# One condition for the pairs and singles that rarely run, and two weight pieces behind the last tile's divisions

## The chip, the cores and the metric

The kernel runs on one core of one Trainium2 chip. The metric is the device time of one launch in microseconds (us), as the median of several runs. The core's engines are named as in the profile: PE is TensorE (matmuls; PEld its weight loads), DVE is VectorE, ACT is ScalarE, POOL is GpSimd and SP is SyncE, which issues most DMA transfers.

## The reference

One sequence of 2048 tokens with 512 features goes through two blocks, each behind a layer norm without weights, each added to its input. The first is linear attention with 32 heads of 16 features and a learned feature map (two softmaxes per head). The second is a mixture of 8 experts, of which each token takes one:

```python
h = x + _A_ref(_layernorm(x, axis=-1), A_wqkv, A_w_phi, A_wo)
h2 = h + _B_ref(_layernorm(h, axis=-1), B_w_gate, B_w1, B_w2)
```

```python
logits = xf @ w_gate
topk_idx = jnp.argsort(-logits, axis=-1)[:, :K]      # K = 1
gates = _softmax(topk_val, axis=-1)                  # of one value
...
h = _silu(xf @ w1[e]) @ w2[e]                        # 512 -> 1792 -> 512
out = out + w * h
```

All is float32. The kernel computes an expert for the tokens routed to it only. How many those are is known when the router has run: with these inputs 103, 594, 80, 127, 286, 222, 239 and 397.

## The kernel before

**Precision.** A float32 value is split into a high part (line 89, ScalarE copies it into a shorter format) and a low part (line 92, or 252 for weights: VectorE subtracts the high part from the value). A product is three matmuls: high by high (L95), high by low (L96), low by high (L97). So each weight chunk that arrives costs one pass of ScalarE and one of VectorE, and each group of matmuls reads both.

**Stages.** The profile's order of time is: attention's features up to about 177 us; the output stage up to about 265; and the experts. The output stage is a loop over 16 tiles of 128 tokens, with its steps staggered: `s_num` (attention's numerator and denominator, divided on VectorE at L573 and L574 into `o`), `s_ot` (transposes of `o` into the bank `pto`, split into `xh` and `xl`), `s_wo` (output projection, bank `po`; then `hb`, the sum with the input, and `lg`, the logits; its statistics at L1022 and L1025 on ScalarE with `hnm` on POOL between them), `s_rank` and `s_inv` (place of each token in its expert, `ivT`). The first expert's weights are already split in that loop, in quarter pieces (`hi_piece`, `lo_piece`); the table `LOS` says in which round of the loop the low pieces of a chunk come.

**Experts.** The largest expert's tokens go as one unit of 128 and one wide group of 468, a second and a third expert in wide groups of 400 and 288 (WN). What is left goes in pairs (up to 256 rows of one expert, two tiles of 128) and singles (128 rows). The program's order is: unit 0, wide group of 468, pair 1, pair 2, pairs 3 to 8 if there are so many, WN, single 0, wide group of 400, single 1, singles 2 to 7 if there are so many. With these inputs two pairs and three singles are live, so pairs 3 to 8 are jumped over and single 2 runs inside its condition. A conditional block is fallen into where it runs; where it doesn't, each engine compares and jumps behind it.

**Preparing the next unit.** A unit makes the next one ready while it runs: it gathers its rows from DRAM (`rows`, `gather`; POOL, L180), normalizes them (`ahead`, VectorE, L207), transposes them on TensorE (`turned`, L214, tile `mtr`) and splits the result (`xhi`, `xlo`); it also splits the next weight chunks (`step`, `split`) and asks for the ones behind (`fetch`, `load`, on SP). Where the next unit may not exist, `split` and `fetch` stand under small conditions on flags that each engine loads into a register (`load_fl`, `load_flags`). Since pair q may be followed by another pair, each pair does this for pair q + 1 with no condition on the transposes, and `keep(q)` stores what the result of pair q needs: the row numbers, and the rows themselves in a second pair of buffers. The result (`pair_result`, L1424) is written by the unit that comes next.

**What sets the order.** The program is written once; a scheduler orders each engine's instructions by the durations that it expects and by explicit ties (`after(x)`: issue not before x; `pin` holds the last instruction of a kind). So an instruction moved in the text can reorder its neighbours on other engines. A bank of PSUM is reused in turn: a matmul into a bank waits for the engine that reads the bank's earlier content.

## Time and profile before

| | us |
|---|---|
| median of 3 runs | 620.19 (619.78 to 621.09) |
| profiled execution | 619.78 |
| its span, first to last instruction | 618.0 |
| mean granted clock of TensorE | 0.998 |
| busy in the span: TensorE | 609.5 |
| VectorE | 441.6 |
| ScalarE | 354.5 |
| GpSimd | 240.5 |

A line of a timeline reads: start in us, duration in us, engine, line of the kernel, operation, tile written <- tiles read, shape, and in brackets the idle time of the engine ahead of it with what ended it. Matmuls overlap in the pipeline, so the cost of one is best read from one start to the next. A line of waits gives engine, operation and line, what it waited for, the total in us, how often, and the longest. In a table of windows each engine has its busy time in the window.

### The profile page before, as it was taken

Reading aid. Unit: us, or ns where it says so; the run is one execution under the profiler, and the core shown is the slowest. Engines: PE = TensorE matmul, PEld = TensorE weight load, DVE = VectorE, ACT = ScalarE, POOL = GpSimd, SP = SyncE. Lnnn points to the kernel's source line nnn. Section 1 sums busy time; section 2 is a strip of 40 time slices with the busy share of each in tenths; the row PEclk is TensorE's granted clock in tenths of the full one; section 3 lists DMA queues with packets and bytes.
Section 4 is the critical chain, followed back from the end, with each engine's and each line's share of the span. In section 5 each row is a group of like instructions: output and inputs, shape, how many; then the busy total and the mean of one; then the engine's idle time right before and its main releaser. Section 6 shows DMA issues by size and latency. Waiting matters only on the chain. (4 is left out here: it accounts for less than half of the span.)

```text
span 618.0 us, 13816 instructions
## 1 busy us (share of the span) xinstructions
PE 609.5 (99%) x5213; PEld 545.4 (88%) x5213; DVE 441.6 (71%) x938; ACT 354.5 (57%) x626; POOL 240.5 (39%) x333
## 2 busy tenths in 40 slices
PE   9999999999999999999999999999999999999996
PEld 8888888888889999888888898888899889999885
DVE  7988787878898878886534557776555784346893
ACT  6666676667535546873234546666456655645771
POOL 3577688868716645541110022240301430010440
PEclk9999999999999999999999999999999999999999
DMA  8711111110103249531078267574755594444931
GB/s 317 264 37 53 52 52 53 54 53 19 36 4 99 74 150 399 206 109 56 21 275 326 69 239 313 200 251 151 248 196 175 174 336 157 136 171 141 326 127 39
DMA packets 25121, 95.12 MB, mean 154 GB/s; under 512 B 3838, under 2 KB 3838, under 8 KB 17873
## 3 DMA queue, kind: packets, MB, share of 16 engines
q1 hardware_dynamic: 20624, 80.81, 37.0%
q0 software_dynamic: 4272, 13.28, 6.4%
q8 instruction: 44, 0.72, 0.5%
q14 instruction: 37, 0.29, 0.1%
q10 hardware_dynamic: 144, 0.02, 0.0%
HBM read 85.68 MB, written 8.65 MB: 153 GB/s over the span
## 5 line engine op out<-in xcount | busy, mean ns | idle before, releaser
L252 DVE TENSOR_TENSOR wlo<-raw,whi 128x1024 fp32r<-128x1024 f32 (+1 forms) x119 | 135.2, 1159 | 29.4 <-ACT whi L89 28.4
L89 ACT ACTIVATE whi<-raw 128x1024 fp32r<-128x1024 f32 (+1 forms) x120 | 115.2, 992 | 8.2 <-DMA raw<-in_w_dram 5.1
L180 POOL DMA_INDIRECT xg<-hbuf,gidx x26 | 34.1, 1312 | 126.4 <-DVE xn L207 48.6
L95 PE MATMUL gw<-zx,whi 128*128 128x240 f32 (+3 forms) x212 | 69.6, 328 | 0.9 <-issue 0.7
L97 PE MATMUL gw<-zx,wlo 128*128 128x240 f32 (+3 forms) x212 | 68.1, 321 | 0.0
L96 PE MATMUL gw<-zx,whi 128*128 128x240 f32 (+3 forms) x212 | 68.1, 321 | 0.0
L711 POOL TENSOR_TENSOR ph<-t,sm 128x1024 f32<-128x1024 f32 x32 | 62.1, 1942 | 12.6 <-DVE sm L709 12.3
L92 DVE TENSOR_TENSOR hA<-hs,hA 128x240 fp32r<-128x240 f32 (+3 forms) x57 | 26.7, 469 | 50.4 <-ACT hA L89 49.1
L1376 ACT ACTIVATE hs<-gw 128x468 f32<-128x468 f32 (+2 forms) x39 | 19.2, 491 | 72.4 <-PE gw L97 72.4
L95 PE MATMUL yt<-hA,whi 128*128 128x468 f32 (+2 forms) x168 | 56.7, 338 | 0.0
L97 PE MATMUL yt<-hA,wlo 128*128 128x468 f32 (+2 forms) x168 | 56.7, 338 | 0.0
L703 ACT ACTIVATE t<-t,rstd 128x1024 f32<-128x1024 f32 x32 | 36.9, 1152 | 34.0 <-DVE t L702 31.0
L708 DVE TENSOR_REDUCE sm<-t 128x64 f32<-128x1024 f32 x32 | 38.8, 1212 | 7.4 <-ACT t L703 5.3
L95 PEld LDWEIGHTS gw<-zx,whi 128*128 128x128 f32 x212 | 39.9, 188 | 3.6 <-ACT hs L1376 1.0
L96 PEld LDWEIGHTS gw<-zx,whi 128*128 128x128 f32 x212 | 40.0, 189 | 1.4
L97 PEld LDWEIGHTS gw<-zx,wlo 128*128 128x128 f32 x212 | 39.9, 188 | 1.3
L95 PE MATMUL po<-wohi,xh 128*128 128x260 f32 x128 | 37.5, 293 | 0.6 <-DVE cum L1045 0.6
L96 PE MATMUL yt<-hA,whi 128*128 128x288 f32 (+2 forms) x116 | 37.8, 325 | 0.0
L97 PE MATMUL po<-wohi,xl 128*128 128x260 f32 x128 | 36.5, 285 | 0.0
L96 PE MATMUL po<-wolo,xh 128*128 128x260 f32 x128 | 36.1, 282 | 0.0
L89 ACT ACTIVATE hA<-hs 128x240 fp32r<-128x240 f32 (+3 forms) x70 | 33.4, 478 | 2.2
L197 POOL DMA_INDIRECT out_dram<-xg,sidx x12 | 14.4, 1202 | 50.1 <-DVE xg L1401 28.2
(490 smaller groups left out, 1783.1 us busy)
## 6 DMA issues: line engine op xcount, KB each, us to landing
raw<-in_w_dram SPq DMA_DIRECT2D x56, 1024.0 KB
xt<-in_x_dram SPq DMA_DIRECT2D x32, 256.0 KB
xT<-in_xTs_dram SPq DMA_DIRECT2D x16, 256.0 KB
hbuf<-hb SPq DMA_DIRECT2D x6, 515.0 KB
hbuf<-hb SPq DMA_DIRECT2D x2, 514.0 KB
phT<-in_wv_dram SPq DMA_DIRECT2D x4, 256.0 KB
phT<-in_wqkT_dram SPq DMA_DIRECT2D x4, 256.0 KB
phT<-in_wqkT_dram SPq DMA_DIRECT2D x2, 512.0 KB
```

Of the source, the lines that this page charges most:

```text
L89: return A.activation(dst, src, AF.Copy)
L92: return V.tensor_tensor(dst, src, hi.bitcast(F32), op=OP.subtract)
L95: T.matmul(ps, ahi, bhi, start=first, stop=False)
L96: T.matmul(ps, ahi, blo, start=False, stop=False)
L97: return T.matmul(ps, alo, bhi, start=False, stop=last)
L180: G.indirect_dma_start(out=dst[0:n, :], out_offset=None, in_=hbuf if col or tab is gidS else hbuf[0:S // 2, :], in_offset=bass.IndirectOff ...
L197: m = G.indirect_dma_start(out=out, out_offset=bass.IndirectOffsetOnAxis(ap=tab[0:n, col:col + 1], axis=0), in_=src[0:n, 0:D], in_offset=N ...
L252: return eng.tensor_tensor(lo, r, h.bitcast(F32), op=OP.subtract)
L703: pin["ex"] = A.activation(t, t, AF.Exp, scale=st[c]["rstd"])
L708: V.tensor_reduce(sm, t, AX.X, OP.add)
L711: pin["f2"] = G.tensor_tensor(ph.rearrange("p (a f) -> p a f", f=DH), t, bc(sm, DH), op=OP.mult)
L1376: A.activation(h, p, AF.Silu)
```

## The change

Three things change. Pairs 3 to 8 and singles 3 to 7 go together into one outer condition at the program's end; single 2 loses its condition (it now always runs), and the late pairs become a plain function, `late_pair`, that prepares nothing ahead. Since no pair follows pair 2 any more, pair 2 makes no rows ready for a third, `keep` is gone, pair 2 splits and fetches WN's weights with no condition, and `pair_result` reads the rows where pair 2 had gathered them. Single 2 makes no rows ready for a fourth (a later single would do that for itself). And in the output stage the low pieces (1, 0) and (1, 1) leave the table `LOS` and come in the last round but behind that tile's divisions (`on`) and the low part `xl`.

```diff
@@ -1142,7 +1142,7 @@
             V.tensor_tensor(est16, est16, pidx, op=OP.subtract)
             V.tensor_scalar(selS, iotaN[:, 1:5], est16, None, op0=OP.is_equal)
 
-        LOS = {NT - 4: range(0, 2), NT - 3: range(2, 4), NT - 2: range(4, 6), NT - 1: range(6, 8)}
+        LOS = {NT - 4: range(0, 2), NT - 3: range(2, 4), NT - 1: range(6, 8)}
         for c in range(NT + 8):
             if c > 1:
                 at(s_num, c)
@@ -1218,6 +1218,10 @@
                          NT - 1: ((2, 0), (2, 1), (2, 2), (2, 3))}.get(c, ()):
                 with after(st[c - 2]["sq"] if c == NT - 4 else st[c - 1]["oT"][2]):
                     hi_piece(k, i, 4)
+            if c == NT - 1:
+                with after(st[c]["on"]), after(pin["xl"]):
+                    lo_piece(1, 0, 4)
+                    lo_piece(1, 1, 4)
             if c in LOS:
                 with after(st[c - 2]["lg"]), after(st[c - 2]["hp"]):
                     for i in LOS[c]:
@@ -1312,13 +1316,10 @@
         flags[u] = (mo, nx_)
 
     def fetch(u, c):
+        if 1 < u < NQ:
+            load(c, we[0] if u == 2 else we[2])
+            return
         mo, nx_ = flags[u]
-        if 1 < u < NQ:
-            with tc.If(mo == 2):
-                nc.sync.dma_start(raw[c], w12_at(we[2], c))
-            with tc.If(mo == 1):
-                nc.sync.dma_start(raw[c], w12_at(nx_, c))
-            return
         with tc.If(mo > 0):
             nc.sync.dma_start(raw[c], w12_at(nx_, c))
 
@@ -1410,7 +1411,7 @@
 
     def pair_result(q):
         for t in range(2):
-            result(LC + 1 + t, pl[0][:, t, :], xg[2 + t], pair_n(q, t))
+            result(2 * q + t, pl[0][:, t, :], xg[2 * (q == 1) + t], pair_n(q, t))
 
     def last_result(r=None):
         if yl:
@@ -1431,7 +1432,7 @@
     def step(c, i, e=None, u=None):
         def f():
             with after(pin["hi"]), after(pin["lo"]):
-                if u is not None and u < NQ:
+                if u is not None and u < 3:
                     split(u, c, i, i + 1)
                 else:
                     half(c, i)
@@ -1518,39 +1519,23 @@
             todo[j].append(step(c, i, None, q + 1))
             if j == 12:
                 todo[j].append(step(2, 1, None, q + 1))
-        def keep(q):
-            G.tensor_copy(sidx[:, LC + 1:LC + 3], sidx[:, 2 * q:2 * q + 2])
-            if q > 1:
-                for t in range(2):
-                    rows(xg[2 + t], 2 * q + t, pair_n(q, t))
-
         if q == 1:
             for j, (c, i) in ((2, (5, 0)), (3, (5, 1)), (5, (6, 0)), (6, (6, 1))):
                 todo[j].append(step(c, i, None, q))
         else:
             for i in range(6):
                 todo[i].append(step(4 + i // 2, i % 2, None, q))
-        if q < NP:
+        if q == 1:
             todo[0].append(lambda: gather(q + 1))
             todo[9].insert(0, lambda: ahead(0))
             todo[10][0:0] = [lambda: turned(0), lambda: ahead(1)]
             todo[11].insert(0, lambda: turned(1))
-        if True:
-            todo[8 if q == 2 else 4].append(lambda: keep(q))
-        if 3 <= q + 1 <= NP:
-            todo[4].append(lambda: tc.mark_branch_hint_location(
-                f"p{q + 1}", hint=smin(smax(vals["p"] - 2 * q, 0), 1),
-                engines=[ENG.PE, ENG.DVE, ENG.Activation, ENG.Pool, ENG.SP]))
         for j, fs in (hooks or {}).items():
             todo[j] = fs + todo[j]
-        load_flags(q + 1)
         if q > 1:
             for c in (2, 3):
                 fetch(q, c)
-        if q > 1:
             pair_result(q - 1)
-        if q == 2:
-            V.memset(pl[0][P - 32:P, 1, :], 0.0)
         for j in range(NJ + 1):
             if j < NJ:
                 c, o = j // 4, j % 4 * P
@@ -1571,9 +1556,44 @@
             for f in todo[j]:
                 f()
             if q == 1 and j == 4:
-                load_fl(2, NQ)
+                load_fl(2, 3)
         for t in range(2):
             g2(NJ - 1, t)
+
+    def late_pair(q):
+        e = nc.values_load(flg[96:97, q:q + 1], engines=[ENG.SP], min_val=0, max_val=E - 1)
+        for c in range(NW):
+            load(c, e)
+        ring = hA.rearrange("p a b -> p (a b)")
+        rh = [ring[:, i * PT:(i + 1) * PT] for i in range(3)]
+        rl = [ring[:, (3 + i) * PT:(4 + i) * PT] for i in range(3)]
+        x = xhi[0], xlo[0]
+        for t in range(2):
+            v = slice(t * P, t * P + P)
+            rows(xg[2 + t], 2 * q + t)
+            norm(xg[2 + t], V)
+            turn(x[0][:, :, v], x[1][:, :, v])
+        for c in range(NW):
+            split_chunk(c)
+        py = [pss.tile([P, 512], F32, name="py", tag="s") for _ in range(2)]
+        for j in range(NJ):
+            c, o = j // 4, j % 4 * P
+            p = bank("gw")[:, 0:PT]
+            for k in range(KD):
+                mm3(p, w1_at(whi, c, k)[:, o:o + P], w1_at(wlo, c, k)[:, o:o + P], x[0][:, k, :], x[1][:, k, :],
+                    k == 0, k == KD - 1)
+            h = hs[j % 2][:, 0:PT]
+            A.activation(h, p, AF.Silu)
+            hi_of(rh[j % 3], h)
+            lo_of(rl[j % 3], h, rh[j % 3])
+            for t in range(2):
+                v = slice(t * P, t * P + P)
+                mm3(py[t], rh[j % 3][:, v], rl[j % 3][:, v], w2_at(whi, j), w2_at(wlo, j), j == 0, j == NJ - 1)
+        for t in range(2):
+            result(2 * q + t, py[t], xg[2 + t])
+
+    def more():
+        return smax(vals["s"] - 3, vals["p"] - 4)
 
     def single(r):
         def g2(py, j0, j1):
@@ -1589,6 +1609,9 @@
             last_result(r)
         if r == 1:
             rows(own(2), SB + 2)
+        if r > 2:
+            norm(own(r), V)
+            turn(*single_x(r))
         for c in range(4):
             si = silu(c, gemm1(single_x(r), c))
             if c:
@@ -1621,9 +1644,9 @@
                 with after(pin["hi"] if c else si), after(pin["lo"] if c else None):
                     split_chunk(4 + c)
                 fetch(f, 4 + c)
-        if 1 < r + 1 < NS:
+        if 2 < r + 1 < NS:
             with after(pin["g1"]), after(pin["hi"]), after(pin["lo"]):
-                tc.mark_branch_hint_location(f"s{r + 1}", hint=smin(smax(vals["s"] - (r + 1), 0), 1),
+                tc.mark_branch_hint_location(f"s{r + 1}", hint=smin(smax(more() if r == 2 else vals["s"] - (r + 1), 0), 1),
                                            engines=[ENG.PE, ENG.DVE, ENG.Activation, ENG.Pool, ENG.SP])
         if r == 1:
             yl.append(psw.tile([P, 2, 512], F32, name="yl", tag="w")[:, 0, :])
@@ -1663,6 +1686,12 @@
         if r + 1 < NS:
             load_flags(f + 1)
             jp = 5
+            if r > 1:
+                with after(pin["hi"]), after(pin["lo"]):
+                    for c in range(4):
+                        split_fetch(f + 1, c)
+                g2(py, 2, NJ)
+        if 1 < r + 1 < 3:
             with after(pin["hi"]), after(pin["lo"]):
                 n = norm(own(r + 1), V)
             with after(pin["hi"]), after(n):
@@ -1673,7 +1702,7 @@
                 for c in range(1, 4):
                     split_fetch(f + 1, c)
             g2(py, jp, NJ)
-        else:
+        elif r + 1 == NS:
             g2(py, 2, NJ)
         if r < NS - 2:
             rows(own(r + 2), SB + r + 2)
@@ -1783,10 +1812,6 @@
     pair(2, {0: [call(rows, src[t], WC + t, WT[t][1]) for t in (2, 0, 1)],
              3: [call(wide_n, 2)], 4: [call(wide_n, 0)], 5: [call(wide_x, 2), call(wide_n, 1)], 6: [call(wide_x, 0)],
              7: [call(wide_x, 1)]})
-    with ExitStack() as ictx:
-        for q in range(3, NP + 1):
-            ictx.enter_context(tc.If(np_v > 2 * (q - 1), preferred_fallthrough_block=True, label=f"p{q}"))
-            pair(q)
     ew0, ew1, es0, es1 = we[0:4]
     xr = ([xg[0], raw[2][:, KD * WN:KD * WN + ROW], xg[3]],
           [xg[0], xn2[0], xg[3], xg[2]])
@@ -1802,7 +1827,7 @@
     load_flags(NQ)
     for c in (2, 3):
         load(c, es0)
-    pair_result(NP)
+    pair_result(2)
     wide({
         0: [call(rows, xg[1], SB)],
         1: [step(4, 0)], 2: [step(4, 1, es0)], 3: [step(5, 0)], 4: [step(5, 1, es0), call(rows, xg[2], WC + 3)],
@@ -1830,10 +1855,16 @@
         half(4, 1)
     fetch(NQ + 1, 4)
     single(1)
-    with ExitStack() as ictx:
-        for r in range(2, NS):
-            ictx.enter_context(tc.If(ns_v > r, preferred_fallthrough_block=True, label=f"s{r}"))
-            single(r)
+    single(2)
+    with tc.If(more() > 0, preferred_fallthrough_block=True, label="s3"):
+        with ExitStack() as ictx:
+            for r in range(3, NS):
+                ictx.enter_context(tc.If(ns_v > r, preferred_fallthrough_block=True, label=f"t{r}" if r == 3 else f"s{r}"))
+                single(r)
+        with ExitStack() as ictx:
+            for q in range(3, NP + 1):
+                ictx.enter_context(tc.If(np_v > 2 * (q - 1), preferred_fallthrough_block=True, label=f"p{q}"))
+                late_pair(q)
     V.tensor_copy(final, sidx[:, LC:LC + 1])
     G.tensor_copy(seen, xg[0][:, D:D + 1])
     for c in range(NW):
```

In the output stage the order of VectorE changes like this, at the divisions of the last tile (- before, + after; `wlo_3697` is the low part of chunk 1):

```order
 L1034 TENSOR_REDUCE tmx<-lg 128x2
-L252 TENSOR_TENSOR wlo_3697<-raw_3522,whi_3696 128x512
+L573 RECIPROCAL den<-pn 128x16
 L1036 TENSOR_TENSOR eq<-lg,tmx 128x16
 L1048 TENSOR_REDUCE gt<-tmx 128x2
-L252 TENSOR_TENSOR wlo_3697<-raw_3522,whi_3696 128x512
+L574 TENSOR_TENSOR o<-pn,den 128x256
```

The first reciprocal and the first division move ahead of the two pieces, which now stand, four in a row with the two that followed, behind the sums `hb` of tile 13.

On ScalarE, a little later in the same stage (`whi_3698` and `whi_3700` are high parts of chunks 2 and 3; L1022 and L1025 are tile 13's statistics, `xh` is the last tile's):

```order
-L89 ACTIVATE whi_3698<-raw_3523 128x512 x4
-L89 ACTIVATE xh<-pto 128x512
-L1022 ACTIVATE junk,hsum<-hb 128x512
-L89 ACTIVATE whi_3700<-raw_3524 128x512
-L1025 ACTIVATE junk,hsum<-hb,hnm 128x512
+L89 ACTIVATE whi_3698<-raw_3523 128x512 x3
+L1022 ACTIVATE junk,hsum<-hb 128x512
+L89 ACTIVATE whi_3698<-raw_3523 128x512
+L1025 ACTIVATE junk,hsum<-hb,hnm 128x512
+L89 ACTIVATE xh<-pto 128x512
```

The last tile's `xh` moves behind tile 13's two statistics.

On TensorE in pair 2, at one of the two places where it transposed for pair 3 (`pl` is pair 2's output, `gw` its hidden layer):

```order
 L96 MATMUL pl<-wlo_4550,hA 112x512
 L97 MATMUL pl<-whi_4549,hA 112x512
-L214 MATMUL mtr<-ident,xn_3704 128x128 x4
 L95 MATMUL gw<-zx,whi_3698 128x240
-L1326 UNCONDITIONAL_BRANCH
 L96 MATMUL gw<-zx,whi_3698 128x240
 L97 MATMUL gw<-zx,wlo_3699 128x240
```

Four transposes go, and the matmuls close up.

## The prediction

> **What bounds the kernel now.** I read the page's busy shares first, then the table of windows, then the waits of TensorE, and last the instruction timeline at each place where the change acts.
>
> ```profile
> PE 609.5 (99%) x5213; PEld 545.4 (88%) x5213; DVE 441.6 (71%) x938; ACT 354.5 (57%) x626; POOL 240.5 (39%) x333
> ```
>
> ```profile
> core 0: us, PE busy (x) PEld busy (x) DVE busy (x) ACT busy (x) POOL busy (x), PEclk, DMA share, GB/s
> 245.00:260.00 15.00, 14.37 (x111) 13.06 (x110) 14.12 (x71) 13.43 (x31) 8.01 (x21) 1.00 0.72 266
> 260.00:275.00 15.00, 15.00 (x84) 12.16 (x83) 13.20 (x31) 11.17 (x17) 8.38 (x8) 1.00 0.34 96
> 395.00:435.00 40.00, 39.88 (x265) 34.78 (x263) 28.55 (x40) 26.58 (x47) 9.88 (x8) 1.00 0.59 205
> 435.00:481.00 46.00, 45.13 (x339) 44.88 (x340) 26.06 (x33) 26.29 (x44) 7.04 (x7) 1.00 0.65 223
> ```
>
> TensorE is busy for all but 8.5 us of the span, at a granted clock of 1.00 in these windows. Pair 2 (395 to 435) and the wide group WN (435 to 481) leave VectorE and ScalarE some 30 to 45% idle, so work taken from those two there is worth nothing by itself. The end of the output stage is different: between 245 and 260 VectorE has 0.88 us idle, and between 260 and 275 it has 1.80. So two things count: matmuls that vanish, and the few places where TensorE stands still. Its two longest waits after the start are these:
>
> ```profile
> PE gw L95 <- issue: 0.7, 1, 0.7
> PE po L95 <- DVE cum L1045: 0.6, 1, 0.6
> ```
>
> The change touches the surroundings of both, and of a third, shorter one.
>
> **Pair 2's transposes.** Pair 2 prepares rows for a third pair that this routing does not have. The change drops that: two gathers, two normalizations on VectorE, two splits, and two groups of four transposes on TensorE. One group, with the matmuls around it, and the same step without a group four microseconds earlier:
>
> ```profile
> 422.60 0.40 PE L97 MATMUL pl<-whi,hA 128*112 128x512 f32 x1
> 422.83 0.60 PE L214 MATMUL mtr<-ident,xn 128*128 128x128 f32 x4
> 423.19 0.36 PE L95 MATMUL gw<-zx,whi 128*128 128x240 f32 x1
> 423.39 0.27 PE L96 MATMUL gw<-zx,whi 128*128 128x240 f32 x1
> ```
>
> ```profile
> 420.09 0.27 PE L95 MATMUL gw<-zx,whi 128*128 128x240 f32 x1
> 420.20 0.27 PE L96 MATMUL gw<-zx,whi 128*128 128x240 f32 x1
> ```
>
> From start to start the group takes 423.19 − 422.83 = 0.36, and the matmul behind it keeps the next one waiting for 0.20, where the same matmul without a group takes 0.11. So a group costs 0.36 + 0.09 = 0.45, and two cost **0.89**. Nothing hides this: TensorE has no gap on either side. The gathers, normalizations and splits lie beside TensorE and are counted as nothing. If they had been late they would show as a wait, and there is none in the window.
>
> **Single 2's transposes.** The last single makes rows ready for a fourth one that does not come. That drops one group:
>
> ```profile
> 606.90 0.60 PE L214 MATMUL mtr<-ident,xn 128*128 128x128 f32 x4
> 607.25 0.48 PE L96 MATMUL yl<-wlo,hA 128*128 128x512 f32 x1
> 607.57 0.39 PE L97 MATMUL yl<-whi,hA 128*128 128x512 f32 x1
> ```
>
> It takes 0.35, and the first matmul behind it 0.32 where one of 512 columns takes 0.23 (422.60 to 422.83): 0.35 + 0.09 = **0.44**. The condition at the head of single 2 goes too. I find no gap at it on TensorE and count nothing.
>
> **The jump between pair 2 and WN.** The skipped pairs 3 to 8 stand there now. TensorE, ScalarE and VectorE each compare and jump.
>
> ```profile
> 434.48 0.40 PE L97 MATMUL pl<-whi,hA 128*112 128x512 f32 x1
> 435.18 0.37 PE L95 MATMUL mh<-zx,whi 128*128 128x288 f32 x1 [0.30 <-PEq L1786]
> ```
>
> From 434.48 to 435.18 is 0.70, where such a matmul takes 0.23 (422.60 to 422.83 above): the jump costs TensorE **0.47**. VectorE must also read pair 2's sums before WN's second bank is free; in the new order I give at most 0.1 of this back, inside the range. Some four microseconds later TensorE stands still again, behind ScalarE:
>
> ```profile
> 438.29 0.29 PE L97 MATMUL gw<-zx,wlo 128*128 128x288 f32 x1
> ...
> 439.88 0.40 PE L95 MATMUL gw<-zx,whi 128*128 128x288 f32 x1 [0.69 <-issue]
> ```
>
> ```profile
> 437.54 0.44 ACT L89 ACTIVATE hA<-hs 128x288 fp32r<-128x288 f32 x1
> 439.42 0.41 ACT L1376 ACTIVATE hs<-gw 128x288 f32<-128x288 f32 x1 [1.44 <-PE gw L97]
> ```
>
> The gw matmul at 439.88 starts when the activation from 439.42 ends (439.83). That activation could start when its input was there: the last matmul for it began at 438.29 and took 0.29, so at about 438.6, and ScalarE had been free since 437.98. It came 0.84 later. The same step of the first wide group, where no jump lies ahead, did not:
>
> ```profile
> 284.05 0.37 PE L97 MATMUL gw<-zx,wlo 128*128 128x468 f32 x1
> ```
>
> ```profile
> 284.46 0.56 ACT L1376 ACTIVATE hs<-gw 128x468 f32<-128x468 f32 x1 [1.30 <-PE gw L97]
> ```
>
> There ScalarE starts 0.04 after its input's end (284.42). My reading is that ScalarE's instructions after the jump came late. The trace doesn't show instruction arrival, so this is an inference. If ScalarE came at 438.7 it would end at 439.1, before TensorE's stall begins (439.88 − 0.69 = 439.19). The gain lies between 0 (the stall has another cause) and 0.69; I take **0.55**, nearer to the row of the wide group.
>
> [...]
>
> **The output stage.** Two low pieces (the 128x512 subtraction at L252) now run behind VectorE's divisions for the last tile.
>
> ```profile
> 244.45 0.68 DVE L252 TENSOR_TENSOR wlo<-raw,whi 128x512 fp32r<-128x512 f32 x1
> ...
> 246.33 0.41 DVE L574 TENSOR_TENSOR o<-pn,den 128x256 f32<-128x256 f32 x1
> ```
>
> ```profile
> 245.97 0.28 PE L96 MATMUL po<-wolo,xh 128*128 128x260 f32 x1
> 246.89 0.36 PE L95 MATMUL po<-wohi,xh 128*128 128x260 f32 x1 [0.64 <-DVE cum L1045]
> ```
>
> TensorE's po at 246.89 waits for a bank that the division (246.33 to 246.74) reads out: 0.92 where such a step takes 0.12, so 0.80 lost. Without the two pieces (0.60 each to the next start) that division ends near 245.2, and the 0.80 goes. But ScalarE's order changes with it. The high part xh of the last tile goes behind three operations that stood after it:
>
> ```profile
> 245.99 0.72 ACT L1025 ACTIVATE junk<-hb,hnm 128x512 f32<-128x512 f32 x1 [0.36 <-POOL hnm L1024]
> ...
> 249.50 0.58 ACT L89 ACTIVATE xh<-pto 128x512 fp32r<-128x512 f32 x1
> 249.97 0.62 ACT L1022 ACTIVATE junk<-hb 128x512 f32<-128x512 f32 x1
> ...
> 251.11 0.71 ACT L1025 ACTIVATE junk<-hb,hnm 128x512 f32<-128x512 f32 x1
> ```
>
> In the new order ScalarE comes to L1022 one piece earlier than xh now, at about 249.05, to L1025 between 250.2 and 250.6 (1.14 behind it, as here, or 0.4 more where it waits for POOL's mean, as the earlier tile's at 245.99 did), and to xh between 250.9 and 251.3. It is done between 251.4 and 251.9.
>
> ```profile
> 252.00 0.36 PE L95 MATMUL po<-wohi,xh 128*128 128x260 f32 x1
> ```
>
> This matmul, the first of the last tile, now starts at 252.00; without the 0.80 TensorE would reach it at 251.2, and so it waits 0.2 to 0.7. Most of the gain is given back. I take **0.25** net, from 0.80 (xh early enough) to −0.5 (xh at its late end and xl, VectorE's part behind it, late as well).
>
> **Loads of flags.** One flag for pair 3 is now read beside the first read in the wide stage, not eight in pair 1: two register loads, on engines with idle time there. Nothing. POOL's scatters of pair 2 no longer stand behind two gathers. The gather into xg[1] for single 0 now waits for pair 2's scatter; its rows are not touched before the ninth of WN's sixteen steps.
>
> **Sum.** 0.89 + 0.44 + 0.47 + 0.55 + 0.25 = 2.60. The profiled execution took 619.78 with a span of 618.0, 1.8 around it. 619.78 − 2.60 = 617.2. The median of the three runs is 620.19, 0.4 above that execution, so I predict a median of **617.6**.
>
> **Rivals.** First, *only the instructions count*: the three stalls are only moved, to ScalarE's xh, to the bank that VectorE must free, and to the next activation. For it speaks that the stalls follow from other engines' order, which stays much as it is; against it, that the wide group without a jump has no such stall. 0.89 + 0.44 and about 0.2 of the jump make 1.5: 618.7 in the median.
>
> Second, *VectorE becomes the bound up to unit 0's end*. It has no slack there:
>
> ```profile
> 278.12 1.10 DVE L92 TENSOR_TENSOR zx<-mtr,zx 128x512 fp32r<-128x512 f32 x2
> ```
>
> ```profile
> 279.31 0.44 PE L96 MATMUL mh<-zx,whi 128*128 128x468 f32 x1
> ```
>
> The two end at 279.22, 0.09 before the matmul that reads the last. VectorE's idle time from 245 to 275 is 0.88 + 1.80 = 2.68; each microsecond of waiting beyond that is lost on TensorE at 279. The wait for xh alone is 1.6 (xl starts at 250.3 by its place behind xh now, 251.9 at worst). If the ranking and the row index of the last tiles, which follow one from the other, each find VectorE out of other work for as long, it waits 4.8 and is 2.1 late. Against that stand 1.33 + 0.47 of gains, so the kernel is 0.3 slower: 620.5. It decides from 1.8 beyond the slack. Against it: four low pieces, 2.4 us of work, now lie behind the divisions and fill the first of these waits.
>
> Third, *all waits vanish*: 0.89 + 0.44 + 0.47 + 0.69 + 0.80 = 3.29, 616.9. Against it stands ScalarE's new order.
>
> Fourth, *the change doesn't do what it says*: a block meant to be skipped runs, for which pair 2's 40 us are the nearest price (about 658), or the jump that is left at the end costs what the one in the middle did (1.0 more, 618.6). No matmul stands behind that one.
>
> **How the numbers follow.** Forecast 0.58 (617.0 to 618.3), only instructions 0.20 (618.3 to 619.2), VectorE the bound 0.10 (619.2 and up), all waits vanish 0.10 (616.4 to 617.0, since a stall can cost more than the idle time shown), not as it says 0.02. A difference below 0.2%, 1.24 us, cannot be told from none here, so faster means below 618.95. Faster: 0.58 + 0.10 + half of the first, 0.10, gives 0.78. Slower, above 621.4: half of the second and half of the last, 0.06. The same: the rest, 0.16. The range from 616.4 to 619.3 holds the forecast, the third rival and nearly all of the first.
>
> **What would show it.** TensorE's work falls by 12 transposes, 1.33 us. No wait at WN's first matmul, and the activation of WN's second chunk starts within 0.2 of its input: right on the jump and on ScalarE; if the activation is still late, the stall was not the jump's. In the output stage the po wait is gone, and a shorter one stands before the first po matmul of the last tile. The forecast is wrong if TensorE's waits in 245 to 280 sum to over 1 us, or if a new wait follows WN's start.

## The result, and the profile after

The changed kernel takes **629.51 us** in the median (628.69 to 630.25, four runs). The kernel before took 620.36 beside it (619.78 to 621.09, four runs). The ratio is 1.0147, with a 95% interval from 1.0129 to 1.0164: 9.2 us slower, where 2.6 us faster were forecast. The profiled execution took 629.61, with a span of 627.9 and a mean granted clock of 0.989.

The busy times of the page, changed kernel:

```profile
PE 610.7 (97%) x5201; PEld 546.3 (87%) x5201; DVE 438.0 (70%) x931; ACT 352.8 (56%) x623; POOL 232.3 (37%) x327
```

The 12 transposes are gone, as forecast. TensorE is nevertheless busy for 1.2 us longer, in a span that is 9.9 us longer. Its waits, beside the warm-up at the start, are now a single one:

```profile
PE mtr L214 <- issue: 9.8, 1, 9.8
```

The po wait, the gw wait and the wait for the jump that the prediction spoke of have all left this list. In their place stands one that is six times as long as those three together (0.6, 0.7 and 0.3). It lies in single 1, near the end. TensorE's timeline there, changed kernel:

```profile
581.60 0.40 PE L97 MATMUL yl<-whi,hA 128*128 128x512 f32 x1
591.81 1.09 PE L214 MATMUL mtr<-ident,xn 128*128 128x128 f32 x4 [9.82 <-issue]
592.55 0.78 PE L95 MATMUL yl<-whi,hA 128*128 128x512 f32 x1
593.12 0.63 PE L96 MATMUL yl<-wlo,hA 128*128 128x512 f32 x1
```

The same place before:

```profile
584.01 0.40 PE L97 MATMUL yl<-whi,hA 128*128 128x512 f32 x1
584.48 0.63 PE L214 MATMUL mtr<-ident,xn 128*128 128x128 f32 x4
...
585.17 0.40 PE L96 MATMUL yl<-wlo,hA 128*128 128x512 f32 x1
```

These are the transposes of single 2's normalized rows, which single 1 prepares. From the matmul ahead of them to the transposes it is 591.81 − 581.60 = 10.21 instead of 584.48 − 584.01 = 0.47, so the stall costs **9.74**. The view names "issue", that is, nothing that it can name. VectorE, which writes the tile `xn` that they read, has the reason in its own timeline (changed kernel, then before):

```profile
591.16 0.55 DVE L207 TENSOR_SCALAR xn<-xg 128x512 f32<-128x512 f32 x1 [9.71 <-DMA out_dram<-xn,sidx]
```

```profile
583.82 0.55 DVE L207 TENSOR_SCALAR xn<-xg 128x512 f32<-128x512 f32 x1
```

The normalization ends at 591.71 and the transposes start 0.10 later. It waits because `xn` still holds result rows of the wide group of 400, and the scatter of these to DRAM (L197, on GpSimd's queue) has not read them all yet. So the question is why that scatter is late. GpSimd's timeline, changed kernel:

```profile
570.76 2.34 POOL L197 DMA_INDIRECT out_dram<-xg,sidx  x1 [0.31 <-issue]
573.41 0.98 POOL L180 DMA_INDIRECT xg<-hbuf,gidx  x1 [0.31 <-DMA out_dram<-xg,sidx]
579.86 1.49 POOL L180 DMA_INDIRECT xg<-hbuf,gidx  x1 [5.47 <-DMA out_dram<-xg,sidx]
581.66 1.01 POOL L197 DMA_INDIRECT out_dram<-xn,sidx  x1 [0.31 <-DVE hA L92]
```

Before:

```profile
573.16 2.35 POOL L197 DMA_INDIRECT out_dram<-xg,sidx  x1 [0.30 <-issue]
576.00 0.98 POOL L180 DMA_INDIRECT xg<-hbuf,gidx  x1 [0.49 <-DMA out_dram<-xg,sidx]
577.29 1.72 POOL L197 DMA_INDIRECT out_dram<-xn,sidx  x1 [0.30 <-DVE hA L92]
...
588.47 1.40 POOL L180 DMA_INDIRECT xg<-hbuf,gidx  x1 [0.31 <-issue]
```

A second gather (L180) now stands between the first gather and the scatter of `xn`. Before, that gather came at 588.47, behind the two scatters. It writes a buffer, `xg[3]`, that the scatter issued at 570.76 is still reading, so GpSimd waits 5.47 for it, and everything behind it in GpSimd's queue waits too. The scatter of `xn` follows the first gather by 8.25 us (581.66 − 573.41) instead of 1.29 (577.29 − 576.00).

GpSimd's order of instructions shows the move. The tile names with numbers are buffers: `xg_4548` is `xg[3]`, `xn_3704` is `xn2[0]` (what the profile calls `xn`). Before:

```order
L197 DMA out_dram<-xg_4547,sidx 2048x512
L197 DMA out_dram<-xg_4548,sidx 2048x512
L180 DMA xg_4547<-hbuf,gidx 128x515
L1322 UNCONDITIONAL_BRANCH
L197 DMA out_dram<-xn_3704,sidx 2048x512
L197 DMA out_dram<-xg_3702,sidx 2048x512
...
L1833 COMPARE_AND_BRANCH
L1626 ISA
L1883 BRANCH_PREFETCH_HINT
L180 DMA xg_4548<-hbuf,gidx 128x515
```

Now:

```order
L197 DMA out_dram<-xg_4547,sidx 2048x512
L197 DMA out_dram<-xg_4548,sidx 2048x512
L180 DMA xg_4547<-hbuf,gidx 128x515
L1323 UNCONDITIONAL_BRANCH
L180 DMA xg_4548<-hbuf,gidx 128x515
L197 DMA out_dram<-xn_3704,sidx 2048x512
L197 DMA out_dram<-xg_3702,sidx 2048x512
```

The `COMPARE_AND_BRANCH` at L1833 is the condition that single 2 stood in. The gather behind it is single 2's own: with `rows(own(r + 2), ...)` every single asks for the rows of the single after next, while there may be one. For single 2 that is single 4, which this routing does not have. With the condition gone, the scheduler was free to put this gather of rows that nobody reads ahead of two scatters that somebody waits for.

A second loss follows from the stall. The table of windows, changed kernel:

```profile
core 0: us, PE busy (x) PEld busy (x) DVE busy (x) ACT busy (x) POOL busy (x), PEclk, DMA share, GB/s
570.00:582.00 12.00, 11.99 (x67) 9.84 (x66) 10.47 (x12) 8.83 (x14) 5.61 (x5) 1.00 0.89 310
...
586.50:591.50 5.00, 0.00 (x0) 0.00 (x0) 0.34 (x1) 0.00 (x0) 0.00 (x0) 0.50 0.66 257
592.00:596.50 4.50, 4.50 (x13) 3.67 (x13) 4.22 (x5) 3.57 (x5) 0.94 (x1) 0.50 0.23 62
```

Narrower windows put the granted clock at 0.50 from 586.35 to 596.59, for 10.24 us, of which TensorE has work in the last 4.8 (from 591.81). In that time it falls back further. At the transposes it is 591.81 − 584.48 = 7.33 behind the kernel before. At a matmul behind the slow stretch it is 599.59 − 590.05 = 9.54 behind: another **2.2**. The four transposes above take 1.09 instead of 0.63. That matmul in the changed kernel, and before:

```profile
599.59 0.39 PE L96 MATMUL yl<-wlo,hA 128*128 128x512 f32 x1
```

```profile
590.05 0.40 PE L96 MATMUL yl<-wlo,hA 128*128 128x512 f32 x1
```

The clock is still at 1.00 up to 586.35, some 4.4 us after the last matmul's end (582.00), and is back at 1.00 from 596.59, 4.8 after TensorE has work again (591.81). A stall of 2.90 us in one of the runs below was followed by a clock of 0.50 too.

### The profile page after: what moved, and what is told of

It is laid out like the page before. It is cut to its first block, busy times and chain, and to the rows that moved or that the text cites. A ratio compares the mean times of both kernels' runs of the same rounds, so it can differ in the third digit from the quotient of the medians.

```text
span 627.9 us, 13583 instructions
## 1 busy us (share of the span) xinstructions
PE 610.7 (97%) x5201; PEld 546.3 (87%) x5201; DVE 438.0 (70%) x931; ACT 352.8 (56%) x623; POOL 232.3 (37%) x327
## 4 chain that ended last, share of the span: by engine, by line
PE 88%; DMA 6%; issue 2%; DVE 1%; ACT 1%; POOL 1%; SPq 0%; POOLq 0%; ACTq 0%
PE gw L95 6%; PE gw L97 6%; PE gw L96 6%; DMA out_dram<-xg,sidx 5%; PE yt L96 4%; PE yt L95 4%; PE yt L97 4%; PE pn L569 3%; PE ptq L770 3%; PE po L95 3%; PE po L97 3%; PE pq L95 2%; PE pk L95 2%; PE po L96 2%; PE pq L96 2%; PE pk L96 2%
## 5 line engine op out<-in xcount | busy, mean ns | idle before, releaser
L180 POOL DMA_INDIRECT xg<-hbuf,gidx x22 | 28.2, 1283 | 90.6 <-DMA out_dram<-xg,sidx 30.6
L197 POOL DMA_INDIRECT out_dram<-xg,sidx x12 | 14.1, 1178 | 72.2 <-DVE xg L1425 39.4
```

What stands on the lines that cost most here:

```text
L180: G.indirect_dma_start(out=dst[0:n, :], out_offset=None, in_=hbuf if col or tab is gidS else hbuf[0:S // 2, :], in_offset=bass.IndirectOff ...
```

## The experiments

None of the kernels leaves a part of the result out. Where a gather is dropped, it moves into a block that does not run with these inputs. Kernels compared in one go share a chip and the runs of the kernel before, whose median stands in brackets beside each. It was 619.99 for the first group and between 618.62 and 618.75 for the later ones, so kernels of different groups are compared by their ratios.

**Without the gather for single 4.** The change, with this one gather left to single 3, which starts each late single's preparation anew.

```diff
+        if r == 3:
+            rows(own(4), SB + 4)
         if r > 2:
             norm(own(r), V)
 ...
-        if r < NS - 2:
+        if r < NS - 2 and r != 2:
             rows(own(r + 2), SB + r + 2)
```

> The change, but single 2's gather of rows for single 4 (into xg[3]) is left to single 3, which does not run here. Theory (queue): without its condition, single 2's gather was scheduled into POOL's queue ahead of the scatter of xn; it waits for the scatter of xg[3], and everything behind it on POOL waits with it, so xn came free late and VectorE's normalization for single 2 too. Then TensorE's wait of 9.8 before single 2's transposes is under 0.5, the granted clock stays at 1.00, and the median is 617.4 (620.36 less the 2.4 that the change was ahead before that wait and the 0.5 behind it). Rival (landing): the scatter of xn lands late because of the weight transfers beside it, wherever the gather stands: TensorE still waits 4 or more and the median is 622 or more.

Measured: 617.76 (before: 619.99), ratio 0.9970, from 0.9958 to 0.9982. GpSimd's timeline, and VectorE's, of this kernel:

```profile
573.62 0.99 POOL L180 DMA_INDIRECT xg<-hbuf,gidx  x1 [0.38 <-DMA out_dram<-xg,sidx]
574.91 1.82 POOL L197 DMA_INDIRECT out_dram<-xn,sidx  x1 [0.30 <-DVE hA L92]
```

```profile
581.50 0.54 DVE L207 TENSOR_SCALAR xn<-xg 128x512 f32<-128x512 f32 x1
```

The scatter of `xn` follows the first gather by 1.29 again, VectorE does not wait, and the stall and the slow clock are gone (TensorE has no wait before the transposes, and the clock is 1.00 from 584 to 596). So the whole loss hung on one gather of rows that nobody reads. The same kernel once more beside others:

> The kernel without the misplaced gather once more, beside the two below. TensorE's trace of it was 2.8 ahead of the kernel before at the last matmul, of which 0.9 lay in pair 2's transposes, 0.5 in the jump, 0.7 in ScalarE's late activation and 0.5 in single 2's transposes: a ratio of 0.9955 if the profiled execution of the kernel before is a usual one; 0.998 (the 1.4 us of vanished transposes alone) if its stalls are not there in most executions.

Measured: 617.66 (before: 618.75), ratio 0.9984, from 0.9975 to 0.9993. The gain is smaller here; the reason comes below.

**The gather kept, behind the scatters.** This separates the gather's place from its existence.

```diff
-            rows(own(r + 2), SB + r + 2)
+            with after(pin["row"] if r == 2 else None):
+                rows(own(r + 2), SB + r + 2)
```

Here `pin["row"]` is the copy of the row numbers that GpSimd makes behind the scatter of single 1's result.

> The change, with single 2's gather for single 4 kept but tied on POOL behind the result scatter of single 1. Queue theory: the place in the queue is all that counts; as the kernel without the gather, 617.4, TensorE's wait under 0.5. Rival (traffic): the gather's own transfer and its wait for xg[3] delay others wherever it is issued: between 619 and 629.

Measured: 618.29 (619.99), ratio 0.9971, from 0.9960 to 0.9982. The gather's work costs nothing that shows; its place in the queue did. VectorE still waits a little in this kernel:

```profile
582.13 0.55 DVE L207 TENSOR_SCALAR xn<-xg 128x512 f32<-128x512 f32 x1 [0.30 <-DMA out_dram<-xn,sidx]
```

So there is no slack to speak of between this scatter and the normalization, even in a good order: TensorE waits 0.4 before the transposes here, and 0.5 in the kernel with the old table `LOS` below.

**The kernel before, with single 2 alone set free.** If the border is the cause, this small edit must bring the whole loss into the old kernel.

```diff
-        if 1 < r + 1 < NS:
+        if 2 < r + 1 < NS:
 ...
+    single(2)
     with ExitStack() as ictx:
-        for r in range(2, NS):
+        for r in range(3, NS):
```

> The kernel before with one edit: single 2 stands outside its condition (and its branch hint is gone). Queue theory: the condition was what kept the gather behind the two scatters, so the wait appears here as well: 8 to 10 on TensorE before single 2's transposes, a lower granted clock behind it, 630 to 633. Rival (the wait comes from the missing pair work or from the loads of flags): no such wait, 620.4 as before.

Measured: 630.17 (619.99), ratio 1.0167, from 1.0151 to 1.0182. GpSimd's and TensorE's timelines:

```profile
575.86 0.98 POOL L180 DMA_INDIRECT xg<-hbuf,gidx  x1 [0.54 <-DMA out_dram<-xg,sidx]
580.62 1.81 POOL L180 DMA_INDIRECT xg<-hbuf,gidx  x1 [3.78 <-DMA out_dram<-xg,sidx]
582.74 1.01 POOL L197 DMA_INDIRECT out_dram<-xn,sidx  x1 [0.30 <-DVE wlo L252]
```

```profile
592.67 0.66 PE L214 MATMUL mtr<-ident,xn 128*128 128x128 f32 x2 [8.46 <-issue]
```

Nothing else of the change is in this kernel, and the stall is there, with a granted clock of 0.50 for about 6.8 us (589.2 to 596.0). The other waits of before (po 0.6, gw 0.6, jump 0.3) are there too.

**The change, with single 2 in a condition that is true.** The reverse of the last edit: the rest of the change stays.

```diff
-    single(2)
-    with tc.If(more() > 0, ...):
+    with tc.If(smax(vals["s"] - 2, vals["p"] - 4) > 0, preferred_fallthrough_block=True, label="s2"):
+        single(2)
+        with tc.If(more() > 0, ...):
```

> The change with single 2 back inside a condition (one that holds here), the late singles and pairs nested in it. Queue theory: the block's border keeps single 2's gather behind the two scatters, so no wait of 9.8; and the condition itself costs TensorE nothing, as the prediction said: 617.8, like the kernel without the gather. Rival: entering the condition costs TensorE 0.3 or more, 618.3 or above.

(Its branch hint comes back with it.) Measured: 617.72 (618.62), ratio 0.9987, from 0.9978 to 0.9996, and no wait of TensorE behind the warm-up. The gather for single 4 is behind both scatters (574.59 and 576.76) again:

```profile
585.45 1.36 POOL L180 DMA_INDIRECT xg<-hbuf,gidx  x1 [0.30 <-issue]
```

So the condition that was taken away costs TensorE nothing that can be seen, as the prediction had it, but it did work as a border for the order.

**The late gather left in place, the normalized rows put elsewhere.** This tests the last link: if VectorE waits because `xn` is still being read, another buffer ends the wait though the scatter stays late.

```diff
-                n = norm(own(r + 1), V)
+                n = norm(own(r + 1), V, xg[2])
 ...
-                xh, xl = turn(*single_x(r + 1))
+                xh, xl = turn(*single_x(r + 1), None, xg[2])
```

(`xg[2]` would hold the rows for single 3; the gather for these is left to single 3, which does not run.)

> The change with the misplaced gather left where it is, but single 2's normalized rows go into xg[2] and not into xn (single 3's gather, which would overwrite xg[2], is left to single 3, which does not run here). Queue theory: the scatter of xn is still late by some 7, but nothing waits for it any more; no wait on TensorE before single 2's transposes, and the time is that of x1_again within 0.5. Rival (the rows of single 2 themselves, or another transfer behind the gather, come late): the wait stays, 627 or more.

Measured: 617.30 (618.75), ratio 0.9978, from 0.9969 to 0.9988. GpSimd and TensorE:

```profile
579.35 1.77 POOL L180 DMA_INDIRECT xg<-hbuf,gidx  x1 [6.51 <-DMA out_dram<-xg,sidx]
581.42 1.09 POOL L197 DMA_INDIRECT out_dram<-xn,sidx  x1 [0.30 <-DVE hA L92]
```

```profile
581.74 0.63 PE L214 MATMUL mtr<-ident,xg 128*128 128x128 f32 x4
```

The gather still waits 6.51, the scatter of `xn` is as late as in the changed kernel (581.66), and TensorE passes at 581.74 without a wait. The chain is shown link by link: border gone, gather ahead, scatter late, buffer not free, normalization late, transposes late. Its median is the lowest of all, and its interval lies below 1, but it overlaps that of the kernel without the gather in the same group (0.9975 to 0.9993). It also has one gather less, the one for single 3.

**The output-stage part alone, and all but it.** The first is the kernel before with the two low pieces moved; the second is the kernel without the gather for single 4, with the old table `LOS`.

```diff
-        LOS = {NT - 4: range(0, 2), NT - 3: range(2, 4), NT - 2: range(4, 6), NT - 1: range(6, 8)}
+        LOS = {NT - 4: range(0, 2), NT - 3: range(2, 4), NT - 1: range(6, 8)}
 ...
+            if c == NT - 1:
+                with after(st[c]["on"]), after(pin["xl"]):
+                    lo_piece(1, 0, 4)
+                    lo_piece(1, 1, 4)
```

> The kernel before with the output-stage part of the change alone. From the trace of the change: TensorE is 1.25 ahead at the second half of tile 13's projection and 0.39 ahead at the first wide group. So 0.39 faster, 620.0. Rival (the rest of the gain is lost further on): no difference, 620.4, or slower.

Measured: 619.53 (619.99), ratio 0.9996, from 0.9987 to 1.0005. In its trace the wait behind ScalarE at WN is 1.4, twice that of before, so this trace says little of the net.

> The kernel without the misplaced gather (x1), with the output stage as before. TensorE's trace of the change is 0.39 ahead at the first wide group: so 0.4 slower than x1, 618.15. Rival: the output part is worth the whole 0.80 of the wait that it removes, 618.5; or nothing, 617.8.

Measured: 617.59 (618.62), ratio 0.9986, from 0.9977 to 0.9995; the po wait of 0.6 is back. Neither shows a difference that can be measured. That agrees with a net of 0.25, which is 0.04% of the time, and can't confirm it; what there is for it is the pair of traces read below.

**The jump put back.** The kernel without the gather for single 4, with one late pair again in a condition between pair 2 and WN; and the same with all six.

```diff
+    with tc.If(np_v > 4, preferred_fallthrough_block=True, label="p3"):
+        late_pair(3)
 ...
-            for q in range(3, NP + 1):
+            for q in range(4, NP + 1):
```

> The kernel without the misplaced gather (x1), plus a condition with one late pair in it between pair 2 and WN, with its branch hint as before; it is jumped over. The prediction's reading: the jump costs TensorE about 0.5 at WN's first matmul and, through ScalarE's late activation, another 0.6 four microseconds later: 617.76 + 1.1 = 618.9. Rival (the late activation had another cause, the work of the third pair's preparation): only the 0.5 comes back, 618.3.

Measured: 618.17 (618.62), ratio 1.0005, from 0.9991 to 1.0019. By the medians that is 0.5 slower than the kernels of its group without the jump (617.72 and 617.59), as the rival had it, but the intervals overlap. Three of its twelve runs lie between 620.57 and 621.65 and the others from 617.47 to 618.68; the profile is of a run at 617.55, so what the three lost is not shown. The trace is the better evidence for the jump's size. From the last pl matmul to the first mh matmul it is 433.53 − 432.83 = 0.70 again, as before; without the jump, in the second run of the kernel without the gather, it is 433.43 − 433.20 = 0.23. The wait behind TensorE's sequencer is back, in the view of waits:

```profile
PE mh L95 <- PEq L1821: 0.3, 1, 0.3
```

> The kernel without the misplaced gather, with all six late pairs in conditions between pair 2 and WN, where the change had moved them from, with the branch hint. With one late pair there the jump cost TensorE 0.3 to 0.5 at WN's first matmul but ScalarE's activation was not late. If the distance of the jump matters, the second activation of WN is late again by 0.7 and the time is 1.1 above x1_again; if not, only the 0.4 at the first matmul shows, and the late activation came from pair 2's work for a third pair or was chance.

Measured: 624.66 (its runs lie between 622.23 and 625.31; before: 618.75), ratio 1.0091, from 1.0078 to 1.0105. Neither outcome that was expected came: it is 7.0 above the kernel without the gather, by the medians. The 0.3 at the jump is no larger than with one pair, so the loss doesn't lie there. The stall at single 2 is back, with no gather in the way:

```profile
574.54 0.99 POOL L180 DMA_INDIRECT xg<-hbuf,gidx  x1 [1.33 <-DMA out_dram<-xg,sidx]
575.83 2.00 POOL L197 DMA_INDIRECT out_dram<-xn,sidx  x1 [0.30 <-DVE wlo L252]
```

```profile
584.35 0.55 DVE L207 TENSOR_SCALAR xn<-xg 128x512 f32<-128x512 f32 x1 [2.79 <-DMA out_dram<-xn,sidx]
```

VectorE waits 2.79, TensorE stands for 2.90, and about 3.4 us at a granted clock of 0.50 follow (586.2 to 589.6). The scatter's issue ends 1.1 later than in the kernel without the gather (577.83 against 576.73), and its transfer takes longer: 6.52 from there until VectorE starts, against at most 4.77 (581.50 − 576.73). The transfers are slower ahead of it already, since the first gather waits 1.33 instead of 0.38 for a scatter that was issued at the same time (569.66 and 569.69). Why they are slower in this kernel stays open; the trace is of the fastest of its five runs. In neither of these two kernels is the activation behind the jump late: ScalarE is idle for 0.65 and 0.64 ahead of it, and for 1.44 before.

**The late activation.** Before, ScalarE's activation at 439.42 came 0.84 after its input. My theory was that instructions arrive late behind the jump; no trace shows their arrival. If arrival is what counts, four one-column activations ahead of the jump, which shift ScalarE's program, may move the lateness, and the same four behind it must not.

```diff
+                if q == 1 and j == 6:
+                    with after(pin["hi"]):
+                        for _ in range(4):
+                            A.activation(seen, pidx, AF.Copy)
```

(In pair 1. For the second kernel they stand in the wide group of 400, with `n == WU` as the condition.)

> The kernel before with four one-column activations (on ScalarE, their result used by nobody) put into pair 1, so that ScalarE's instructions behind the jump stand four places later in its program. [...] The jump theory: the lateness follows the jump, whatever stands where; the wait stays, 0.6 or more. [...]

> The control: the same four activations, but in the wide group of 400, behind the place. [...]

Measured: 618.71 and 618.62 (both 618.74), ratios 0.9995 (0.9986 to 1.0005) and 0.9998 (0.9988 to 1.0008). The lateness is gone in both. ScalarE's timeline of the first:

```profile
438.36 0.41 ACT L1376 ACTIVATE hs<-gw 128x288 f32<-128x288 f32 x1 [0.64 <-PE gw L97]
```

Since the control lost it too, the shift did not do it. What the profiles show is this: the lateness is there in before and in the two kernels made from it in the first group (where before takes 619.99), with stalls of TensorE of 0.7, 0.6 and 1.4, and it is absent in all four kernels with a jump that ran in the groups where before takes 618.62 to 618.75 (ScalarE is idle ahead of this activation for 1.44, 1.38 and 2.10 in the three, and for 0.63 to 0.65 in the four). It may belong to the chip or the execution, not to the program; what it is stays open. If the kernel before has it on the one chip and not on the others, that would account for much of the difference between a gain of 2.2 (619.99 − 617.76) and one of 1.1 (618.75 − 617.66). No trace of before was taken in the later groups, so this is an inference.

## Why the prediction was wrong

The step that failed stands in the last two sentences on single 2: "The condition at the head of single 2 goes too. I find no gap at it on TensorE and count nothing." The price of the condition itself was right: nothing. What was missed is that it kept single 2's gathers on their side of it. Counted as nothing, its removal cost 9.74 us of stall and 2.21 at half clock. The record shows the new orders of VectorE and ScalarE in the output stage and of TensorE in pair 2; GpSimd's order at single 2, where the gather moved ahead of two scatters, is not in it. No rival named it either. The rival for a slower kernel was put into the output stage, and the closing part looked for a new wait behind WN's start, with nothing said of a place or a size.

The other terms can be read from the moment at which TensorE reaches the same matmul in both traces. TensorE in the changed kernel, at pair 2's transposes, the jump and the late activation:

```profile
422.22 0.39 PE L97 MATMUL pl<-whi,hA 128*112 128x512 f32 x1
422.45 0.27 PE L95 MATMUL gw<-zx,whi 128*128 128x240 f32 x1
422.56 0.27 PE L96 MATMUL gw<-zx,whi 128*128 128x240 f32 x1
...
433.21 0.39 PE L97 MATMUL pl<-whi,hA 128*112 128x512 f32 x1
433.44 0.30 PE L95 MATMUL mh<-zx,whi 128*128 128x288 f32 x1
...
437.20 0.29 PE L95 MATMUL yt<-hA,whi 128*128 128x288 f32 x1
437.47 0.40 PE L95 MATMUL gw<-zx,whi 128*128 128x288 f32 x1
```

The prediction's rows have the first at 422.60 and the third at 423.39: TensorE is 0.38 ahead, and then 0.83, so the group was worth 0.45. The pl matmul at 433.21 came at 434.48 (1.27 ahead) and the mh matmul at 435.18 (1.74 ahead): 0.47 for the jump. The yt matmul at 437.20 came at 438.90 (1.70 ahead), and the last one at 439.88 (2.41 ahead): 0.71 for the late activation.

| where | forecast | measured |
|---|---|---|
| lead when the change begins to act (240) | – | −0.13 |
| output stage, to 279.31 | −0.25 | −0.26 |
| pair 2's transposes | −0.89 | −0.45 − 0.44 |
| the jump | −0.47 | −0.47 |
| given back behind WN's first bank | up to 0.1 | +0.04 |
| late activation | −0.55 | −0.71 |
| single 2's stall | 0 | +9.74 |
| half clock behind it | 0 | +2.21 |
| single 2's transposes | −0.44 | −0.45 |
| behind the last matmul | 0 | +0.81 |
| span | | +9.9 |

In this pair of traces the forecast gains came to 2.7 (0.26 + 0.89 + 0.47 + 0.71 + 0.45, less the 0.04) against 2.6. Take the two terms of the stall away, and the changed kernel would be at 629.51 − 9.74 − 2.21 = 617.6. The kernel without the gather measured 617.76 on a chip where the kernel before takes 619.99. So the sizes held for what was counted, though one of them, the late activation, by luck; the sum left out one thing four times as large, and a smaller one, the 0.81 at the end. On the chip where the kernel before takes 618.75, the gain without the gather was 1.1 and not 2.6. That is near the first rival's 1.5, but not for that rival's reason: the trace of that run has no wait of TensorE over 0.2 behind the warm-up, so no stall was moved elsewhere.

By its steps:

- **The output stage** went much as described. The first division no longer stands behind the two pieces: it ends at 245.01 (the forecast had 245.2; taking 1.20 off 246.74 gives 245.5, and any of these is early enough). ScalarE makes `xh` of the last tile at 250.51, where I had put it between 250.9 and 251.3. TensorE waits 0.14 for it (the first po matmul starts 0.50 behind the transposes, 251.14 − 250.64, instead of 252.00 − 251.64 = 0.36), and 0.15 for `xl` at 251.87: 0.29 in all, within the 0.2 to 0.7 forecast. VectorE's reading at unit 0's end, the place of the second rival, costs TensorE 0.24: the step from 278.47 to 278.92 is 0.45 instead of 0.21 (279.10 to 279.31 before), since VectorE is done at 277.77 + 1.10 = 278.87. VectorE does become the bound there, as that rival said, but it costs 0.24 and not 2.1. ScalarE, TensorE and VectorE of the changed kernel:

```profile
250.51 0.58 ACT L89 ACTIVATE xh<-pto 128x512 fp32r<-128x512 f32 x1
```

```profile
251.60 0.28 PE L96 MATMUL po<-wolo,xh 128*128 128x260 f32 x1
251.87 0.39 PE L97 MATMUL po<-wohi,xl 128*128 128x260 f32 x1
...
278.47 0.38 PE L95 MATMUL mh<-zx,whi 128*128 128x468 f32 x1
278.92 0.48 PE L96 MATMUL mh<-zx,whi 128*128 128x468 f32 x1
```

```profile
277.77 1.10 DVE L92 TENSOR_TENSOR zx<-mtr,zx 128x512 fp32r<-128x512 f32 x2
```

- **The jump** was sized rightly from one start to the next: the step is 0.23 without it and 0.70 where it is put back. The 0.30 behind TensorE's sequencer goes with it and comes back with it (0.3 with one late pair there, and 0.3 with all six).
- **The late activation** is not there in the changed kernel's trace (its activation starts at 437.01, 0.04 behind its input), and 0.71 lies just above the upper end that was given (0.69). The sign named for this came true, and even so the reason, instructions that arrive late behind the jump, got no support: four kernels with a jump have no such lateness. So the gain was right in size in this pair of traces by luck; a kernel with a jump but without the lateness has nothing of it to gain.
- **"Nothing" for GpSimd's scatters of pair 2** was right, and it shows how the mistake was made: the text looks at the queue for what was removed in pair 2, and not for what was freed at the end.

## What to carry to other kernels

Here a condition was also a border that the scheduler didn't move work across. Where one is removed, read the new order of every engine past the place where it stood, the DMA-issuing queues first, and ask of each transfer that moved ahead what it waits for and who stands behind it. A prefetch of data that may not be needed should be tied behind the transfers that somebody waits for, or be left to the block that needs it; and a long stall of TensorE can cost more than its own length, here 2.2 on top of 9.7.

## What the runs showed of the hardware that I had not expected

**A waiting gather held up the scatters behind it in GpSimd's queue.** The 5.47 us of the gather were passed on in full to scatters whose data had been ready (VectorE wrote the rows of `xn` from 572.14 to 572.87). The issues at 573.41, 579.86, 581.66 and 582.97 follow each other as they stand in the order above. The same gather waited 3.78 with single 2 set free, and the scatter of `xn` came behind it there too.

**The same scatter of 128 rows takes 5 us in one kernel and 8 in another.** From the end of its issue to the normalization that waited for it, the scatter of `xn` took 5.16 us when issued at 575.15 (the gather kept behind), 6.52 at 575.83 (all pairs jumped), 8.27 at 582.74 (single 2 set free) and 8.49 at 581.66 (the changed kernel). From the start of the issue it is 6.98, 8.52, 9.28 and 9.50. The two that were issued late took longest, but all four are different kernels. The DMA share from 580 to 585 and from 585 to 590 is 1.02 and 0.85 in the changed kernel, 0.93 and 0.95 with single 2 set free, 1.01 and 0.85 with all pairs jumped, and 0.97 and 1.02 in the kernel before. That other transfers are the reason is an inference; it was not tested by itself.

**The half clock lasted about 3.4, 6.8 and 10.24 us**: 3.4 with the stall of 2.90 (all pairs jumped), 6.8 with 8.46 (single 2 set free) and 10.24 with 9.82 (the changed kernel). The first two are worked out from the mean clocks of windows: 0.70 from 585 to 588 and 0.80 from 588 to 592; 0.92 from 585 to 590, 0.50 from 590 to 595 and 0.90 from 595 to 600. With the stall of 2.90, the clock fell only at about 586.2, when TensorE had been at work again since 585.00. So in this run the slow stretch was longer than the stall; how long a stall must be is not shown.

**The end is 0.8 longer with the new ending.** GpSimd's last scatter, changed kernel, and before:

```profile
623.09 0.99 POOL L197 DMA_INDIRECT out_dram<-xg,final  x1 [9.97 <-DVE xg L1425]
```

```profile
614.01 1.01 POOL L197 DMA_INDIRECT out_dram<-xg,final  x1 [7.79 <-DVE xg L1424]
```

From the end of that issue to the end of the span it is 627.9 − 624.08 = 3.8, and before 618.0 − 615.02 = 3.0. It is 3.8 in the kernel without the gather (616.0 − 612.22), in the one with the old table `LOS` (616.4 − 612.62) and with the normalized rows elsewhere (615.6 − 611.80) as well. The prediction's fourth rival had allowed 1.0 for the jump that is left at the end. But the kernel before jumps over the singles there too, and in the kernel with all pairs jumped no late pair stands behind the end, and it is 3.8 there (620.4 − 616.64). So neither the jump nor the length of the late pairs is shown to be the reason, and the cause stays open. The 0.8 is to be taken off the sum of the gains in these three kernels.
